# Filter loads in one hardware queue in order of use, and the start-up reordered around them, in a fused FFT filter and SwiGLU kernel

## The chip, the cores and the metric

The kernel runs on one core of one Trainium2 chip. The metric is the device time of one execution in microseconds (us). Inside a trace, times count from the start of the span.

Engines: PE is TensorE, DVE is VectorE, ACT is ScalarE, POOL is GpSimd, SP is SyncE, which here only issues DMAs.

## The reference

Eight sequences of 3008 rows of 256 numbers are filtered in the frequency domain. Then each row is normalized and goes through a gated feed-forward layer.

```python
X = np.fft.rfft(x, axis=1)                       # x: 8 x 3008 x 256
y = np.fft.irfft(X * (filt_r + 1j * filt_i), n=3008, axis=1)
x = y.reshape(8 * 3008, 256)
xn = x / np.sqrt(np.mean(x * x, -1, keepdims=True) + 1e-06) * rms_g
g, val = xn @ w_gate, xn @ w_val                 # 256 x 1536 each
out = (silu(g) * val) @ w_out                    # 1536 x 256
```

## The kernel before

The feed-forward matmuls fill PE, which was busy for 99% of the profiled span. The filter of the next sequence is fitted in beside them, but the filter of the first sequence has nothing to hide behind. This **start-up** is what the change rearranges. It goes: load x; a first transform; transposes (`t1_mm`) and copies of their results (`t1_copy`); the second transform (`stage_b`, into PSUM tiles `psb`); products with the filter (`products`); the inverse (`inverses`, into PSUM tiles `pgt`) and its copies to `gT`; second transposes; the norm; and then the first **gate product** on PE.

The filters lie in four groups, with eight frequencies in each partition; each group has a real part `fr[c]` and an imaginary part `fi[c]`. A load writes one half of the partitions, and a copy (`f_dup`) brings the same data to the other half.

```python
def f_load(c, e, eng):          # e: 0 real, 1 imaginary; three DMAs, four for c == 0
    ...
    eng.dma_start(t[p0 + 16:p0 + 63:2, :, :]..., raw(src, ...))          # 24 rows, L506
    for g in range(2):
        eng.dma_start(t[p0 + 1 + 24 * g:p0 + 24 + 24 * g:2, lo:KC, :],   # 12 rows, L509
                      raw(src, ...))
    ...
def f_dup(c, e, eng, lo=0, hi=KC):
    t = (fr, fi)[e][c][:, lo:hi, :]
    a, o = (0, HALF) if e else (HALF, 0)
    if eng is nc.scalar:
        eng.activation(out=t[a:a + HALF], in_=t[o:o + HALF], func=AXT.Copy)   # L519
    elif eng is nc.sync:
        eng.dma_start(t[a:a + HALF], t[o:o + HALF])                           # L521
    else:
        eng.tensor_copy(out=t[a:a + HALF], in_=t[o:o + HALF])                 # L523
```

The inverse writes two PSUM banks for a pair of units. When the pair is complete, the banks are copied out, by ACT for most pairs. Only then can PE start the next pair (in the profile it waited 1.97 us for such a copy before its matmul at 28.02), and these copies stand in ACT's queue among all its other work:

```python
def bit_unit(i):                # called by inverses()
    ...
    if closing:
        for dh in range(2):
            ...
            if pair > 5 and dh:
                nc.vector.tensor_copy(out=dst, in_=src)                       # L579
            else:
                nc.scalar.activation(out=dst, in_=src, func=AXT.Copy)         # L581
```

The order that the kernel before has (A is ACT, G is POOL, S is SP):

```python
for c in range(4):
    f_load(c, 0, nc.sync)
    f_load(c, 1, nc.gpsimd if c < 3 else nc.sync)
...
for g in range(4):
    t1_mm(g)
    t1_copy(g, g == 1)          # second argument: on ACT
stage_b(0, 1, 2, 3)
for g in range(4, 8):
    t1_mm(g)
f_dup(0, 0, A, 0, 2)
f_dup(0, 1, G, 0, 2)
...
f_dup(3, 0, S)                  # the last real group's copy, by DMA
products(4, 7)
f_dup(2, 0, A, 0, 4)
f_dup(2, 0, A, 4, 8)
inverses(2)
...
f_dup(3, 1, A, 0, 4)            # the last imaginary group, first half
...
inverses(6)
f_dup(3, 1, A, 4, 8)            # second half
inverses(7)
```

Of the kernel before, what the change touches and what calls it, by code (L numbers as in the profile page):

```python
# [10 lines left out]
FP32 = mybir.dt.float32  # L11
# [110 lines left out]
def kernel(  # L122
# [11 lines left out]
    nc = tc.nc  # L134
# [16 lines left out]
    up = ctx.enter_context(tc.tile_pool(name="up", bufs=2))  # L151
# [76 lines left out]
    def b_mm(b, i):  # L228
        ps = bank(3 if b else (0, 3, 4, 5)[i % 4], "psb").rearrange("p (a d) -> p a d", a=2)
        if b == 0 and i > 3:  # L230
            nc.tensor.matmul(ps[:, 0, :], wz[:, 0:P], wz[:, 0:D], start=True, stop=True)
        for u in range(2):
            k = 2 * i + u
            if b:
                w, t = late_p["wb"], st[b]["t2"][k // KC][:, k % KC, :]
            else:
                w, t = wbp, st[0]["t2"][k // 4][:, k % 4, :]
            nc.tensor.matmul(ps[:, u, :], w[:, k, :], t, start=True, stop=True)  # L238
        return ps
# [4 lines left out]
    def b_unit(b, i, ps=None):  # L244
        if ps is None:
            ps = b_mm(b, i)
        f1, f2 = filt(2 * i, 2)
        if b:
            s1 = late_p["sp"].tile([P, 2, D], FP16, tag="s1", name="s1")
            s2 = late_p["sp"].tile([P, 2, D], FP16, tag="s2", name="s2")  # L250
            if summed(b, i):
                nc.vector.tensor_tensor(out=s1, in0=ps, in1=f1, op=ALU.mult)  # L252
                st[b]["s"][i] = (s1, s2, ps, f2)
                return
        elif i % 2:
            s1 = hp.tile([P, 512], FP16, tag="sg", name="sg").rearrange("p (a d) -> p a d", a=2)
            s2 = hhs[(i // 2) % 4].rearrange("p (a d) -> p a d", a=2)
        else:
            ss = xnp.tile([P, 2, 512], FP16, tag="xn", name="ss")
            s1, s2 = (ss[:, e, :].rearrange("p (a d) -> p a d", a=2) for e in range(2))  # L260
        eng = nc.vector
        if (i in (3, 5, 8, 12, 15)) if b else (i in (3, 7, 9, 12)):
            eng = nc.gpsimd
            v = yp.tile([P, 2, 512], FP32, tag="y", name="v")
            v = v[:, 0, :].rearrange("p (a d) -> p a d", a=2)
            nc.scalar.activation(out=v, in_=ps, func=AXT.Copy)
            ps = v
        eng.tensor_tensor(out=s1, in0=ps, in1=f1, op=ALU.mult)
        eng.tensor_tensor(out=s2, in0=ps, in1=f2, op=ALU.mult)  # L269
        st[b]["s"][i] = (s1, s2)  # L270
# [229 lines left out]
    def raw(src, row, ap):  # L500
        return bass.AP(tensor=src.tensor, offset=src.offset + row * D, ap=ap)

    def f_load(c, e, eng):
        lo = 1 if c == 0 else 0
        src, t, p0 = ((filt_r, fr[c], 0), (filt_i, fi[c], HALF))[e]
        eng.dma_start(t[p0 + 16:p0 + 63:2, :, :].rearrange("p a d -> p (a d)"),  # L506
                      raw(src, c * KC, [[64 * D, 24], [1, KC * D]]))
        for g in range(2):
            eng.dma_start(t[p0 + 1 + 24 * g:p0 + 24 + 24 * g:2, lo:KC, :],  # L509
                          raw(src, 64 * (1 + 11 * g) - c * KC - lo,  # L510
                              [[64 * D, 12], [-D, KC - lo], [1, D]]))
        if c == 0:
            eng.dma_start(t[p0 + 1:p0 + 48:2, 0, :], raw(src, 32, [[64 * D, 24], [1, D]]))
# [10 lines that stand above are left out]
# [13 lines left out]
    def t1_mm(g):  # L537
        if g < 6:
            if g % 2 == 0:
                st[0]["t2t"] = t2p.tile([KR, KC, D], FP16, tag="t2", name="t2")  # L540
            dst = st[0]["t2t"][:, 4 * (g % 2):4 * (g % 2) + 4, :]
        else:
            dst = t3p.tile([KR, 4, D], FP16, tag="t3", name="t2")
        st[0]["t2"][g] = dst
        pool, tag = ((psG, "pg"), (psV, "pv"))[g % 2]
        ps = pool.tile([P, 4, D], FP16, tag=tag, name="pt1")
        af = aT.rearrange("p a k -> p (a k)")
        for a in range(4):
            for dh in range(2):
                b0 = dh * H * P  # L550
                src = af[:, b0:b0 + 32 * P].rearrange("p (i k) -> p k i", k=K2)[:, 4 * g + a, :]
                nc.tensor.transpose(ps[:, a, ts(dh, P)], src, ident)
        st[0]["t2ps"][g] = ps

    def t1_copy(g, on_act):
        dst, ps = st[0]["t2"][g], st[0]["t2ps"].pop(g)
        if on_act:
            nc.scalar.activation(out=dst, in_=ps[0:KR], func=AXT.Copy)
        else:
            nc.vector.tensor_copy(out=dst, in_=ps[0:KR])  # L560
# [60 lines left out]
        for i in range(n):  # L621
            nc.tensor.matmul(pw, wz[:, 0:P], wz, start=True, stop=True)

    def gate(ap):

        g = up.tile([1, 1], FP32, tag="gate", name="gate")
        nc.gpsimd.tensor_copy(out=g, in_=ap)

    def w_load(q):
        cols = ts(q, DFF // 3)  # L630
        for src, dst in ((moe_w_gate, wg), (moe_w_val, wv)):
            nc.gpsimd.dma_start(dst[:, :, cols], src.rearrange("(dt p) j -> p dt j", p=P)[:, :, cols])
        nc.gpsimd.dma_start(wo[:, ts(q, JT // 3), :],
                            moe_w_out.rearrange("(jt p) d -> p jt d", p=P)[:, ts(q, JT // 3), :])

    with tc.manual_schedule():
# [28 lines left out]
            zero(fi[c][HALF:P])  # L665
        with nc.allow_non_contiguous_dma(reason="one gain a partition"):
            nc.sync.dma_start(gsb, moe_rms_g.rearrange("(a p) -> p a", p=P))
        for c in range(4):
            f_load(c, 0, nc.sync)
            f_load(c, 1, nc.gpsimd if c < 3 else nc.sync)  # L670

        warm_up(14, 1)
        for g in range(4):
# [11 lines left out]
        A, G, S = nc.scalar, nc.gpsimd, nc.sync  # L685
        st[0]["t2ps"], st[0]["g"], psb = {}, {}, {}

        def products(*units):
            for i in units:
                b_unit(0, i, psb.pop(i))  # L690

        def stage_b(*units):
            for i in units:
                psb[i] = b_mm(0, i)

        def inverses(*units):
            for i in units:
                bit_unit(i)

        for g in range(4):  # L700
            t1_mm(g)
            t1_copy(g, g == 1)
        stage_b(0, 1, 2, 3)
        for g in range(4, 8):
            t1_mm(g)
        f_dup(0, 0, A, 0, 2)
        f_dup(0, 1, G, 0, 2)
        f_dup(0, 0, A, 2, 4)
        f_dup(0, 1, G, 2, 8)
        t1_copy(4, 1)  # L710
        f_dup(0, 0, G, 4, 8)
        products(0)
        stage_b(4)
        products(1)
        stage_b(5)
        t1_copy(5, 1)
        f_dup(1, 1, G)
        products(3)
        f_dup(1, 0, A, 0, 4)
        f_dup(1, 0, A, 4, 8)  # L720
        inverses(0, 1)
        products(2)
        t1_copy(6, 0)
        t1_copy(7, 0)
        stage_b(6, 7)
        f_dup(2, 1, G)
        f_dup(3, 0, S)
        products(4, 7)
        f_dup(2, 0, A, 0, 4)
        f_dup(2, 0, A, 4, 8)  # L730
# [199 lines left out]
```

## Time and profile before

| | before |
|---|---|
| time, median of 3 runs | 887.42 us (886.8 to 888.33) |
| span of the profiled run | 884.9 us |
| first product on DVE | 21.40 us |
| DVE's last product ends | 37.74 us |
| first gate product on PE | 46.25 us |
| last imaginary group landed | 30.74 us |

ACT's timeline. Columns: start, length, engine, line, operation, output and input tiles, shape, count, and in brackets how long the engine sat idle just before, and on whom.

```profile
25.07 2.00 ACT L519 ACTIVATE fr<-fr 64x1024 f32<-64x1024 f32 x2 [0.72 <-DMA fr<-in_filt_r_dram]
28.48 2.00 ACT L519 ACTIVATE fr<-fr 64x1024 f32<-64x1024 f32 x2
31.89 1.06 ACT L519 ACTIVATE fi<-fi 64x1024 f32<-64x1024 f32 x1
```

The second view is the chain of waits (start, length, what).

```profile
31.89 1.06 ACT fi L519
32.95 0.48 ACT v L266
33.43 0.75 ACT gT L581 x2
34.18 0.94 ACT fi L519
35.12 0.76 ACT gT L581 x2
```

From 31.89 on, the chain is ACT's queue: half of the filter group, a PSUM tile for POOL, two bank copies, the other half, two bank copies. DVE's products are not in these lines (the chain has three of them earlier, from 28.07 to 29.88). The SP queue's issue of the last load, three DMAs:

```profile
24.53 0.77 SPq L506 DMA_DIRECT2D fi<-in_filt_i_dram  x1
25.35 1.63 SPq L509 DMA_DIRECT2D fi<-in_filt_i_dram  x2
```

An issue takes about 0.8 us, so the third starts at 26.20.

### The profile page before, as it was taken

Reading aid. Unit: us, or ns where it says so; the run is one execution under the profiler, and the core shown is the slowest. Engines: PE = TensorE matmul, PEld = TensorE weight load, DVE = VectorE, ACT = ScalarE, POOL = GpSimd, SP = SyncE. Lnnn points to the kernel's source line nnn. Section 1 sums busy time; section 2 is a strip of 40 time slices with the busy share of each in tenths; the row PEclk is TensorE's granted clock in tenths of the full one; section 3 lists DMA queues with packets and bytes.
Section 4 is the critical chain, followed back from the end, with each engine's and each line's share of the span. In section 5 each row is a group of like instructions: output and inputs, shape, how many; then the busy total and the mean of one; then the engine's idle time right before and its main releaser. Section 6 shows DMA issues by size and latency. Waiting matters only on the chain.

```text
span 884.9 us, 17466 instructions
## 1 busy us (share of the span) xinstructions
PE 873.1 (99%) x6257; PEld 559.7 (63%) x6257; DVE 678.2 (77%) x1086; ACT 625.1 (71%) x1070; POOL 437.9 (49%) x394
## 2 busy tenths in 40 slices
PE   9799999999999999999999999999999999999997
PEld 6666666666666666766666666666666666666556
DVE  7866777899888877888688887888778887555555
ACT  7877667687677766876677766887667765676444
POOL 7844931646536752676237661376515761155300
PEclk9999999999999999999999999999999999999999
DMA  8696826665643466444735346332443233222202
GB/s 201 125 192 157 169 74 211 143 145 123 191 121 84 106 147 162 104 96 104 197 79 138 84 96 184 95 84 83 104 147 77 66 87 75 73 66 49 72 24 49
DMA packets 80096, 101.44 MB, mean 115 GB/s; under 512 B 8109, under 2 KB 56685, under 8 KB 79561
## 3 DMA queue, kind: packets, MB, share of 16 engines
q1 hardware_dynamic: 69688, 84.23, 34.7%
q0 software_dynamic: 10240, 15.96, 11.7%
q8 instruction: 49, 0.80, 0.4%
q14 instruction: 39, 0.31, 0.1%
q10 hardware_dynamic: 80, 0.13, 0.1%
HBM read 67.67 MB, written 46.78 MB: 129 GB/s over the span
## 4 chain that ended last, share of the span: by engine, by line
PE 94%; DMA 2%; DVE 1%; ACT 1%; POOL 1%; issue 1%; SPq 0%; ACTq 0%; POOLq 0%
PE po L462 27%; PE pg L443 27%; PE pv L443 27%; PE psi L291 3%; PE psb L238 3%; PE psn L323 2%; PE psa L203 2%; DMA fr<-in_filt_r_dram 2%; PE psq L352 1%; POOL xc L188 0%; DVE o L472 0%; ACT gT L581 0%; PE pt L592 0%; DVE hh L448 0%; ACT fi L519 0%
## 5 line engine op out<-in xcount | busy, mean ns | idle before, releaser
L448 DVE TENSOR_TENSOR hh<-pv,sg 128x512 f16<-128x512 f32 (+2 forms) x588 | 392.8, 670 | 188.9 <-ACT sg L447 78.1
L447 ACT ACTIVATE sg<-pg 128x512 f16<-128x512 f32 (+2 forms) x588 | 340.9, 580 | 221.1 <-PE pg L443 211.0
L462 PE MATMUL po<-wo,hh 128*128 128x256 f16 x2244 | 342.2, 272 | 0.7 <-DVE hh L448 0.3
L443 PE MATMUL pv<-xn,wv 128*128 128x512 f16 (+2 forms) x1176 | 339.6, 370 | 0.0
L443 PE MATMUL pg<-xn,wg 128*128 128x512 f16 (+2 forms) x1176 | 339.5, 370 | 0.0
L462 PEld LDWEIGHTS <-hh 128*128 128x128 f16 x2256 | 216.4, 98 | 95.5 <-issue 1.5
L282 POOL TENSOR_TENSOR s<-s,s 128x512 f16<-128x512 f16 x101 | 116.8, 1157 | 231.9 <-DVE s L276 161.3
L443 PEld LDWEIGHTS <-wv 128*128 128x128 f16 x1176 | 114.9, 98 | 128.8 <-issue 0.3
L419 POOL TENSOR_TENSOR xn<-y,rb 128x1024 f16<-128x1024 f32 (+1 forms) x45 | 126.2, 2803 | 43.8 <-DMA rb<-r_tmp 42.5
L443 PEld LDWEIGHTS <-wg 128*128 128x128 f16 x1176 | 111.3, 98 | 13.4 <-issue 0.3
L358 POOL TENSOR_TENSOR rho<-u,mhalf 128x4 f32<-128x4 f32 (+1 forms) x48 | 49.0, 1022 | 62.2 <-DVE u L356 62.0
L296 ACT ACTIVATE t<-psi 96x512 f16<-96x512 f32 x112 | 66.4, 593 | 8.3 <-PE psi L291 3.0
L276 DVE TENSOR_TENSOR s<-psb,fi 64x512 f16<-64x512 f32 x101 | 69.1, 685 | 3.1
L278 DVE SCALAR_TENSOR_TENSOR s<-psb,fi 64x512 f16<-64x512 f32 x101 | 70.0, 693 | 1.4
L329 ACT ACTIVATE y<-psn,gsb 128x512 f32<-128x512 f32 (+1 forms) x94 | 63.8, 679 | 8.1 <-PE psn L323 0.9
L252 DVE TENSOR_TENSOR s<-psb,fr 128x512 f16<-128x512 f32 x101 | 68.8, 681 | 0.0
L343 POOL TENSOR_TENSOR sq<-sq 128x512 f16<-128x512 f16 (+1 forms) x35 | 39.6, 1132 | 37.1 <-ACT sq L335 37.1
L335 ACT ACTIVATE sq<-psn 128x512 f16<-128x512 f32 (+1 forms) x94 | 54.8, 583 | 0.0
L208 ACT ACTIVATE t<-psa 128x512 f16<-128x512 f32 x70 | 41.8, 597 | 5.6 <-PE psa L203 2.1
L291 PE MATMUL psi<-s,wi 128*128 128x256 f16 x238 | 44.3, 273 | 0.0
L238 PE MATMUL psb<-t,wb 96*128 96x256 f16 x224 | 43.0, 272 | 0.3 <-DVE s L269 0.2
L323 PEld LDWEIGHTS <-t 128*128 128x128 f16 x368 | 28.4, 98 | 20.6 <-issue 0.4
(106 smaller groups left out, 527.3 us busy)
## 6 DMA issues: line engine op xcount, KB each, us to landing
out_dram<-o SPq DMA_DIRECT2D x83, 256.0 KB
xc<-in_x_dram POOLq DMA_DIRECT2D x56, 192.0 KB, 6.1
z_tmp<-t SPq DMA_DIRECT2D x28, 384.0 KB
t<-z_tmp SPq DMA_DIRECT2D x28, 384.0 KB
g_tmp<-t SPq DMA_DIRECT2D x56, 192.0 KB
rb<-r_tmp SPq DMA_DIRECT2D x41, 256.0 KB
t<-g_tmp SPq DMA_DIRECT2D x21, 384.0 KB
t<-g_tmp SPq DMA_DIRECT2D x7, 320.0 KB
```

The source lines that it names most:

```text
L238: nc.tensor.matmul(ps[:, u, :], w[:, k, :], t, start=True, stop=True)
L252: nc.vector.tensor_tensor(out=s1, in0=ps, in1=f1, op=ALU.mult)
L276: nc.vector.tensor_tensor(out=s2[a], in0=ps[e], in1=f2[e], op=ALU.mult)
L278: nc.vector.scalar_tensor_tensor(out=s2[a], in0=ps[e], scalar=-1.0, in1=f2[e], op0=ALU.mult, op1=ALU.mult)
L282: nc.gpsimd.tensor_tensor(out=s, in0=s1, in1=s2, op=ALU.add)
L291: nc.tensor.matmul(ps[:, u, :], wi_at(q, 2 * i + u), ss[q][:, u, :], start=(q == 0), stop=(q == n - 1))
L296: nc.scalar.activation(out=st[b]["t3"][c][:, 2 * r:2 * r + 2, :], in_=ps[0:KR], func=AXT.Copy)
L419: nc.gpsimd.tensor_tensor(out=xv, in0=yv, in1=rv.unsqueeze(1).to_broadcast([P, 2, n, P]), op=ALU.mult)
L443: nc.tensor.matmul(ps[:, 0:w], wt[:, dt_, ts(jt, P)], xn[:, dt_, :], start=(dt_ == 0), stop=(dt_ == 1))
L447: nc.scalar.activation(out=sg[:, 0:w], in_=pg[:, 0:w], func=AXT.Silu)
L448: nc.vector.tensor_tensor(out=hh[:, 0:w], in0=pv[:, 0:w], in1=sg[:, 0:w], op=ALU.mult)
L462: nc.tensor.matmul(po[s4 // per][:, s4 % per, :], hh[:, ts(s4, P)], wo[:, jt, :], start=(jt == 0 and s4 % per == 0), stop=(jt == JT - 1 an ...
```

## The change

The intent is to bring the filter groups in the order in which they are used, from one queue, so that the products begin earlier; to start those products between the transposes instead of after them; and to cut the last filter copy by DMA in two, so that the first half lands sooner. The diff, without the removed helper that nothing calls:

```diff
-        for c in range(4):
-            f_load(c, 0, nc.sync)
-            f_load(c, 1, nc.gpsimd if c < 3 else nc.sync)
+        f_load(0, 0, nc.sync)
+        f_load(0, 1, nc.gpsimd)
+        f_load(1, 1, nc.sync)
+        f_load(1, 0, nc.sync)
+        f_load(2, 1, nc.sync)
+        f_load(2, 0, nc.sync)
+        f_load(3, 0, nc.sync)
+        f_load(3, 1, nc.sync)
...
-        for g in range(4):
-            t1_mm(g)
-            t1_copy(g, g == 1)
-        stage_b(0, 1, 2, 3)
-        for g in range(4, 8):
-            t1_mm(g)
+        t1_mm(0)
+        t1_copy(0, 0)
         f_dup(0, 0, A, 0, 2)
         f_dup(0, 1, G, 0, 2)
+        t1_mm(1)
+        stage_b(0, 1)
         f_dup(0, 0, A, 2, 4)
         f_dup(0, 1, G, 2, 8)
-        t1_copy(4, 1)
+        t1_copy(1, 1)
+        t1_mm(2)
+        t1_mm(3)
         f_dup(0, 0, G, 4, 8)
         products(0)
+        stage_b(2, 3)
+        products(1)
+        t1_copy(2, 0)
...
-        f_dup(3, 0, S)
+        f_dup(3, 0, S, 0, 4)
+        f_dup(3, 0, S, 4, 8)
```

More of the change, by code (lines that the diff above doesn't have):

```diff
@@ L622, in warm_up @@
             nc.tensor.matmul(pw, wz[:, 0:P], wz, start=True, stop=True)
-    def gate(ap):
-        g = up.tile([1, 1], FP32, tag="gate", name="gate")
-        nc.gpsimd.tensor_copy(out=g, in_=ap)
     def w_load(q):
@@ L698, in inverses @@
                 bit_unit(i)
-        for g in range(4):
-            t1_mm(g)
-            t1_copy(g, g == 1)
-        stage_b(0, 1, 2, 3)
-        for g in range(4, 8):
-            t1_mm(g)
+        t1_mm(0)
+        t1_copy(0, 0)
         f_dup(0, 0, A, 0, 2)
         f_dup(0, 1, G, 0, 2)
+        t1_mm(1)
+        stage_b(0, 1)
         f_dup(0, 0, A, 2, 4)
         f_dup(0, 1, G, 2, 8)
-        t1_copy(4, 1)
+        t1_copy(1, 1)
+        t1_mm(2)
+        t1_mm(3)
         f_dup(0, 0, G, 4, 8)
         products(0)
+        stage_b(2, 3)
+        products(1)
+        t1_copy(2, 0)
+        for g in range(4, 7):
+            t1_mm(g)
         stage_b(4)
-        products(1)
-        stage_b(5)
-        t1_copy(5, 1)
         f_dup(1, 1, G)
         products(3)
+        t1_copy(4, 1)
+        t1_copy(5, 1)
+        products(2)
+        t1_copy(3, 0)
+        t1_mm(7)
+        stage_b(5)
         f_dup(1, 0, A, 0, 4)
@@ L721 @@
         inverses(0, 1)
-        products(2)
+        stage_b(6)
         t1_copy(6, 0)
         t1_copy(7, 0)
-        stage_b(6, 7)
+        stage_b(7)
         f_dup(2, 1, G)
-        f_dup(3, 0, S)
+        f_dup(3, 0, S, 0, 4)
+        f_dup(3, 0, S, 4, 8)
         products(4, 7)
```

## The prediction

The sum stands: DVE's last product at 37.5 us against 37.74, a gain of about 0.2 us. The first landing at 19.7 is the author's estimate, close to the landing of the same group's third piece (19.73), and that other loads had held up the last piece was not shown. What the trace of the kernel before shows is this: eleven completion records of that last piece came from 18.55 to 19.43 and the last at 20.63; and from 16 to 20 us, with both queues at work, the DMA moved 199 to 213 GB/s, which is 0.20 to 0.21 MB per us. Part 2 counts "waits for the eighth transfer before": in that trace SP began issues at 18.41, 19.35 and 22.39, each 0.02 us after the eighth transfer before it had landed (18.39, 19.33, 22.37). The argument for the second rival took such a lag of a piece's last record for constant, but in the last imaginary group of that trace it was 0.25 to 0.69 us, not 1.20.

> **What bounds the kernel now.** I read the busy shares first, then the chain of waits to find how far the start-up reaches, then the engines' timelines inside it.
>
> ```profile
> span 884.9 us, 17466 instructions
> PE 873.1 (99%) x6257; PEld 559.7 (63%) x6257; DVE 678.2 (77%) x1086; ACT 625.1 (71%) x1070; POOL 437.9 (49%) x394
> PE 94%; DMA 2%; DVE 1%; ACT 1%; POOL 1%; issue 1%; SPq 0%; ACTq 0%; POOLq 0%
> ```
>
> PE is busy for 99% and carries 94% of the chain; the other 6% lies almost wholly ahead of the first gate product, which the PE timeline has at 46.25 us. From there to 884.9 us PE runs without holes, and the change touches no line of that part. So **the change is worth what it moves the first gate product**, one for one. Inside the start-up, windows of five microseconds:
>
> ```profile
> 20.00:25.00 5.00, 4.42 (x64) 4.01 (x63) 4.55 (x8) 3.76 (x6) 4.75 (x5) 1.00 0.85 203
> 25.00:30.00 5.00, 2.54 (x33) 1.91 (x30) 5.00 (x10) 4.88 (x7) 4.86 (x4) 1.00 0.61 140
> 30.00:35.00 5.00, 4.49 (x58) 3.52 (x59) 4.48 (x8) 4.95 (x9) 4.95 (x5) 1.00 0.52 109
> ```
>
> The columns are stretch, length, busy time of PE, its weight loads, DVE, ACT, POOL, then clock, DMA share and GB/s. Between 25 and 35 us PE is the idle one; DVE, ACT and POOL are all full, while the DMA has room. The reader should see three engines at the limit together: time taken from one of them alone is worth little. Now the DVE line by line, whose products end the stage:
>
> ```profile
> 18.62 0.69 DVE L560 COPY t<-pt 96x1024 f16<-96x1024 f16 x1 [0.75 <-PE pt L552]
> 19.66 1.28 DVE L560 COPY t<-pt 96x1024 f16<-96x1024 f16 x2 [0.35 <-PE pt L552]
> 21.40 0.69 DVE L268 TENSOR_TENSOR ss<-psb,fr 128x512 f16<-128x512 f32 x1 [0.45 <-ACT fr L519]
> ...
> 25.00 1.28 DVE L560 COPY t<-pt 96x1024 f16<-96x1024 f16 x2
> ...
> 34.06 0.69 DVE L268 TENSOR_TENSOR sg<-psb,fr 128x512 f16<-128x512 f32 x1 [0.39 <-PE pgt L573]
> ...
> 37.06 0.68 DVE L269 TENSOR_TENSOR hh<-psb,fi 128x512 f16<-128x512 f32 x1
> ```
>
> The products begin at 21.40, after a wait for ACT's copy of the first real filter group to the other half of the partitions, and end at 37.74. Of the 16.34 us, 24 products at a pitch of 0.60 us are 14.4 and two transposed-tile copies (the pair at 25.00) 1.2, so only about 0.7 us are gaps. Three such copies ran before 21.40, when DVE had nothing else to do. That ACT copy waited for the load:
>
> ```profile
> 20.73 1.17 ACT L519 ACTIVATE fr<-fr 64x512 f32<-64x512 f32 x2 [0.56 <-DMA fr<-in_filt_r_dram]
> 19.00 0.57 POOL L509 DMA_DIRECT2D fi<-in_filt_i_dram  x1 [1.39 <-DMA fi<-in_filt_i_dram]
> 19.61 2.05 POOL L523 COPY fi<-fi 64x512 f32<-64x512 f32 x2
> 22.88 1.89 POOL L523 COPY fi<-fi 64x2048 f32<-64x2048 f32 x1
> ```
>
> POOL is held until 19.57 by issuing loads of later imaginary groups. The completion records in the trace put the landing of the first groups at 20.63 (real) and 19.16 (imaginary). [...]
>
> [...]
>
> **The change, part by part.**
>
> 1. **Filters into one queue.** It takes six load issues (second and third imaginary group) of 0.54 to 0.63 us from POOL, 3.5 us, all before 19.57 and beside its waiting. POOL can start its first copy when the imaginary group lands, 19.2 instead of 19.61: 0.4 us earlier. [...] I estimate the landing at 19.7 instead of 20.63. ACT then needs the 0.67 us that now lie between 20.73 and the product at 21.40, so the first product can start at about 20.4, **1.0 us earlier**. The floor is about 19.8: the imaginary group, and first transposes, their copy and two matmuls.
> 2. **The later groups.** The SP queue issues a piece in about 0.8 us, a group of three in 2.4. Waits for the eighth transfer before included, I estimate the issue of the last filter piece at 28.6 (before 26.20) and landings of: second imaginary 21.5, second real 23, third imaginary 25, third real 27, fourth real 29, fourth imaginary 31.4. Their users come at about 22.4 (POOL), 25 (ACT), 26.6 (POOL), 28.8 (ACT), 29.4 (SP) and 31.6 (ACT). Each is in time, the last by little.
> 3. **Copies between products.** All eight tile copies stay on their engines. But of the DVE's three early ones, two now stand after the first products: 2 x 0.60 = **1.2 us come into the full stretch**. ACT's copy of tile 1 (1.02 us) likewise goes behind its first filter copies, against 0.72 us of idle time before 25.07 that goes.
> 4. **Last filter copy in two DMAs.** Before, one 512 KB copy was issued at 29.37 and its increments came at 33.3 to 33.9. The product at 34.06 began then; the 0.39 us before it stands under PE in the view, but that inverse had issued long before, so I put it down to this copy. Halves of 256 KB should land near 32.5 and 33.6, ahead of the users at about 34 and 35: **up to 0.4 us** goes.
> 5. The removed one-element copy helper is never called: nothing.
>
> Sum for DVE: start at 20.4; 24 x 0.60 = 14.4; four copies 2.4; new and old small gaps 0.3 (a wait for the last transposes, which in turn wait for the copy that frees their bank). 20.4 + 14.4 + 2.4 + 0.3 = 37.5, against 37.74. The stretch behind it (inverses, second transposes, norm, first gate product: 8.5 us) is unchanged. **Gain about 0.2 us**, 887.42 to 887.2. POOL's last product ended at 36.90 and should end near 36.3; it isn't the end of the chain.
>
> **Rivals.**
>
> - *The early filter is all that counts.* If the first landing comes down to the floor, products start at 19.9 and end at 37.0: 0.7 us gained, 886.7. For it: the waits at 20.73 and 21.40 show that only data was missing. Against it: x itself was landing until 15.85[...].
> - *The copies cancel or reverse it.* If the landing doesn't move[...], products start at 21.4 as before, with 1.2 us more work behind them: 38.4, so 888.1. [...]
> - *The single queue becomes the bound.* Issue at 2.4 us a group[...] could make the last imaginary group late: ACT's copy at about 31.6 is tight. One or two microseconds late would show at the end as about 0.5 to 1.5 us, 888 to 889. Against it: from the third real group to the fourth imaginary one the trace has a group landing every 1.5 to 2.0 us from that queue alone.
> - *It is all hidden.* ACT and POOL are as full as DVE between 25 and 35 us, so an early product only waits for filter copies later: no change, 887.4.
>
> **Range and chances.** The mechanisms give -0.7 to +1.5 us; the three runs before spread over 886.8 to 888.33. As a change of this kind was likely made because something measured better, I lean slightly below my sum: 887.1, with 885.9 to 888.5 to hold it 8 times in 10. Two per cent are 17.7 us, more than a third of the whole start-up of 46 us, which is out of reach; so within 2% has 0.98.
>
> **What would show it.** Right: the first product on DVE near 20.4 with its wait still for a filter copy; the pair of copies at 19.66 gone and four copies among the products; no wait for a DMA before the product at 34; DVE's last product at 37.0 to 38.0, first gate product within 0.7 us of 46.25. Wrong, if the first product starts before 19.8 or after 21.2; if ACT's copies of the last imaginary group, or POOL's of the second, wait for DMA by over 0.5 us; or if PE shows holes after the first gate product that it hadn't before, which nothing here would explain.

## More of the kernel before

After its first copy ACT waits once, for the second real group, and begins to copy the last imaginary group at 31.89. It doesn't wait there: the group had landed at 30.74.

## The result, and the profile after

| | before | after |
|---|---|---|
| time, median of 4 runs | 887.78 (886.80 to 888.33) | 889.35 (887.98 to 889.75) |
| span of the profiled run | 884.9 | 887.4 |
| first product on DVE | 21.40 | 20.36 |
| last imaginary group landed | 30.74 | 33.53 |
| ACT begins to copy it | 31.89 | 33.61 |
| DVE's last product ends | 37.74 | 38.75 |
| first gate product on PE | 46.25 | 48.75 |
| span less first gate product | 838.65 | 838.65 |

The ratio of the two is 1.0016, with a 95% interval of 0.9999 to 1.0033. A ratio here is the mean time of one kernel's fast runs over that of the other's of the same rounds, so it is not quite the ratio of the medians in the table. In a later set, five runs of the changed kernel had a median of 890.2 against 886.93 of eleven runs before, ratio 1.0028 (1.0016 to 1.0040). So the change costs about 2 us: within 2 per cent, but slower (shown by the second interval; the first still holds 1), and outside the range that was predicted. The profiled runs differ by 2.50 us at the first gate product and by nothing behind it. First the line of the kernel before, then that of the changed one:

```profile
46.25 0.38 PE L443 MATMUL pg<-xn,wg 128*128 128x512 f16 x1
48.75 0.38 PE L443 MATMUL pg<-xn,wg 128*128 128x512 f16 x1
```

The part behind that product isn't equal in every trace: in the 14 of this document it is 838.6 to 839.0 us, but 839.4 in e3_fill and 840.3 in before_again. So the time of a single run depends on more than its start-up.

The page of the changed kernel, its span and busy shares:

```profile
span 887.4 us, 17469 instructions
PE 874.3 (99%) x6257; PEld 561.0 (63%) x6257; DVE 678.1 (76%) x1086; ACT 624.8 (70%) x1070; POOL 434.2 (49%) x388
```

These say nothing of the loss: the busy times are those of before within 1.3 us, but for POOL's, which are 3.7 us lower. The loss is only seen inside the start-up. DVE's timeline:

```profile
20.36 0.69 DVE L268 TENSOR_TENSOR ss<-psb,fr 128x512 f16<-128x512 f32 x1 [1.23 <-ACT fr L519]
...
34.58 0.69 DVE L268 TENSOR_TENSOR sg<-psb,fr 128x512 f16<-128x512 f32 x1 [0.45 <-PE pgt L573]
...
36.87 0.69 DVE L269 TENSOR_TENSOR ss<-psb,fi 128x512 f16<-128x512 f32 x1 [0.30 <-ACT fi L519]
```

The first product begins 1.04 us earlier, as intended. The wait near 34 is still there, and at 36.87 DVE waits for ACT's copy of the last imaginary group, which it didn't before. So to ACT's timeline:

```profile
19.69 1.16 ACT L519 ACTIVATE fr<-fr 64x512 f32<-64x512 f32 x2 [2.31 <-DMA fr<-in_filt_r_dram]
20.88 1.02 ACT L558 ACTIVATE t<-pt 96x1024 f16<-96x1024 f16 x1
22.58 0.61 ACT L266 ACTIVATE v<-psb 128x512 f32<-128x512 f32 x1 [0.69 <-PE psb L238]
...
29.20 2.00 ACT L519 ACTIVATE fr<-fr 64x1024 f32<-64x1024 f32 x2 [0.79 <-DVE hh L269]
...
33.61 1.06 ACT L519 ACTIVATE fi<-fi 64x1024 f32<-64x1024 f32 x1 [1.01 <-DMA fi<-in_filt_i_dram]
```

ACT also starts 1.04 us earlier (19.69 against 20.73). Then it has the tile copy at 20.88, which before lay ahead of its filter copies, and three waits. The one at 29.20 is put down to DVE by the view, but the third real group had landed at 29.10, so I take it as a wait for that load. The wait at 22.58 is a new round trip, as PE's own line shows:

```profile
21.95 0.60 PE L238 MATMUL psb<-t,wbp 96*128 96x256 f16 x4 [1.19 <-ACT t L558]
```

PE waits for ACT's tile copy to make the next second transforms, and ACT waits for these: that is the 0.69 us. And the chain of waits of the changed kernel, where before's had ACT alone:

```profile
28.85 4.68 DMA fi<-in_filt_i_dram
33.53 0.03 ACTq L519
33.56 0.04 issue
33.61 0.06 ACT fi L519
```

The last load's final piece is issued at 28.85 (before 26.20), lands at 33.53, and ACT starts at once. Behind it the chain is the same as before: one `v`, two `gT`, the second half of `fi`, two `gT`.

**The balance of ACT's queue.** From the start of the first filter copy to that of the last imaginary group's copy I take off the time in which ACT waited for loads. What is left is how long this stretch takes with all data there:

| | first copy | waits for loads | rest | last copy |
|---|---|---|---|---|
| before | 20.73 | 0.72 | 10.44 | 31.89 |
| after | 19.69 | 0.79 + 1.01 | 12.12 | 33.61 |

The new order lengthens ACT's stretch by 1.68 us: 1.02 for the tile copy and 0.69 for the round trip, 1.71 together. The early start (-1.04) plus the longer stretch (+1.68) plus the change in load waits (1.80 - 0.72 = +1.08) make +1.72, which is the shift of the last copy.

That leaves 0.78 us of the 2.50, behind this copy: from it to the first gate product the kernel before took 14.36 us, the changed one 15.14. The windows show it. I cut them to 3.41 us, the length of the halved stretch in the changed kernel: there up to its start and from it on, and in the kernel before, whose clock took no such step in the start-up, a stretch at a like place. The columns are those of the prediction's windows. First the kernel before, then the changed one:

```profile
34.35:37.76 3.41, 2.09 (x37) 1.66 (x36) 3.39 (x6) 2.65 (x7) 3.41 (x5) 1.00 0.03 7
```

```profile
33.64:37.06 3.42, 1.70 (x24) 1.14 (x22) 2.66 (x5) 3.42 (x6) 3.37 (x4) 1.00 0.39 85
37.06:40.47 3.41, 3.16 (x37) 2.88 (x36) 1.69 (x3) 2.16 (x6) 3.41 (x5) 0.50 0.27 30
```

In the changed kernel PE's clock is halved from 37.06 to 40.47, right behind a stretch in which PE was busy for 1.70 of 3.42 us, and just where the inverses run. Such halvings also fell on other stretches and on the kernel before, at other places in each trace: 22.30 to 25.71 in a second one of the changed kernel (after_again), 30.50 to 33.91 in a second one of the kernel before (before_again). PE's busy time ahead of them does not tell where they fall: it was 2.05 of 3.41 us before the halving in e4, while in the kernel before a stretch with 1.92 (24.12 to 27.53) was followed by full clock.

### The profile page after: what moved, and what is told of

The parts are those of the page before. It is cut to its first block, busy times and chain, and to the rows that moved or that the text cites. A ratio compares the mean times of both kernels' runs of the same rounds, so it can differ in the third digit from the quotient of the medians.

```text
span 887.4 us, 17469 instructions
## 1 busy us (share of the span) xinstructions
PE 874.3 (99%) x6257; PEld 561.0 (63%) x6257; DVE 678.1 (76%) x1086; ACT 624.8 (70%) x1070; POOL 434.2 (49%) x388
## 4 chain that ended last, share of the span: by engine, by line
PE 94%; DVE 1%; DMA 1%; POOL 1%; ACT 1%; issue 1%; SPq 0%; DVEq 0%; ACTq 0%; POOLq 0%
PE po L462 27%; PE pg L443 27%; PE pv L443 27%; PE psi L291 3%; PE psb L238 3%; PE psn L323 2%; PE psa L203 2%; DMA fr<-in_filt_r_dram 1%; PE psq L352 1%; DMA fi<-in_filt_i_dram 1%; POOL xc L188 0%; DVE o L472 0%; PE pt L592 0%; ACT gT L581 0%; SPq L509 0%
## 5 line engine op out<-in xcount | busy, mean ns | idle before, releaser
L443 PEld LDWEIGHTS <-wg 128*128 128x128 f16 x1176 | 111.3, 98 | 13.4 <-issue 0.3
```

Of the source, the lines that this page charges most:

```text
L443: nc.tensor.matmul(ps[:, 0:w], wt[:, dt_, ts(jt, P)], xn[:, dt_, :], start=(dt_ == 0), stop=(dt_ == 1))
```

## The experiments

**Theory at the start:** the end of the start-up is set by ACT's queue, not by DVE, and in the changed kernel the last imaginary load holds that queue up; the halved clock adds to it. **Rivals:** the new compute order costs the time by itself; or the halved clock is the main cause; or the load is late only because DMA bandwidth is short, so that no queue would help. The first rival became half of the answer. Where a quotation names a theory by a letter, the sentence ahead of it here says in words what was asked.

All trace readings are put together here: one look each, in the order of the section. "Rest" is as above. "To gate" runs from ACT's copy of the last imaginary group to the first gate product. "Halved" is the stretch of halved clock, if any fell between 18 and 46 us.

| run | order | first copy | load waits | rest | last copy | to gate | first gate | halved |
|---|---|---|---|---|---|---|---|---|
| before | old | 20.73 | 0.72 | 10.44 | 31.89 | 14.36 | 46.25 | none |
| after | new | 19.69 | 1.80 | 12.12 | 33.61 | 15.14 | 48.75 | 37.06-40.47 |
| e1_queue_only | old | 20.10 | 2.62 | 10.55 | 33.27 | 14.36 | 47.63 | 29.10-32.52 |
| e2_order_only | new | 20.06 | 0 | 12.19 | 32.25 | 14.35 | 46.60 | none |
| e3_fill | new | 20.67 | 1.16 | 12.17 | 34.00 | 14.36 | 48.36 | none |
| e4_fr3_act_queue | new | 20.32 | 2.08 | 12.22 | 34.62 | 15.35 | 49.97 | 38.98-42.40 |
| e5_fr3_pool_old_order | old | 21.36 | 0.82 | 10.44 | 32.62 | 14.35 | 46.97 | 30.74-34.15 |
| e6_fr3_pool | new | 19.39 | 1.97 | 12.14 | 33.50 | 14.35 | 47.85 | 33.96-37.38 |
| e7_fr3_pool_fill | old | 21.59 | 2.85 | 10.39 | 34.83 | 14.35 | 49.18 | 31.12-34.53 |
| e8_two_pieces_only | old | 20.80 | 0.94 | 10.44 | 32.18 | 14.35 | 46.53 | 29.78-33.19 |
| e9_fi3_half_by_dma | old | 20.79 | 0.53 | 10.43 | 31.75 | 14.15 | 45.90 | 29.57-32.98 |
| e10_no_last_load | new | 18.78 | 1.20 | 12.26 | 32.24 | 14.36 | 46.60 | none |
| after_again | new | 20.54 | 0 | 12.92 | 33.46 | 14.36 | 47.82 | 22.30-25.71 |
| before_again | old | 21.11 | 0.68 | 10.44 | 32.23 | 14.36 | 46.59 | 30.50-33.91 |

Two things hold throughout: "rest" is 10.39 to 10.55 us in the seven with the old order and 12.12 to 12.92 in the seven with the new one. And the last imaginary group landed at 30.15 to 32.13 in the five with the old loads, at 33.20 to 33.93 in the four with the new loads unaltered. The tail is lengthened in the two traces in which the halved stretch lies over the last inverses: in the changed kernel it begins 3.45 us behind the start of the copy and in e4 4.36 us. In e6 it begins 0.46 us behind it, and the tail is 14.35 us. (The waits of e4 and e5 include 0.17 and 0.82 us which the view puts down to other instructions, but a load that the copy needed had landed about 0.1 us before.)

### The queue alone

The kernel before with the new loads and nothing else. It asks whether the loads alone bring the late landing.

```diff
 (kernel before)
-        for c in range(4):
-            f_load(c, 0, nc.sync)
-            f_load(c, 1, nc.gpsimd if c < 3 else nc.sync)
+        f_load(0, 0, nc.sync)
+        f_load(0, 1, nc.gpsimd)
+        f_load(1, 1, nc.sync)
+        ... (the changed kernel's eight lines)
```

> The kernel before with the filter loads moved into one queue and nothing else. Theory A (the SP queue issues a piece every 0.85 us, so the seven groups it now carries end with the last imaginary piece issued at about 28.9 us and landed at about 33.5, and the copy of the last real group can't be issued before 31.2): first product at about 20.9 instead of 21.40 us, ACT's last filter copies wait for DMA until about 33.5, the product near 34 waits until about 35, DVE's last product ends at about 38.7 instead of 37.74; time 1 to 2.5 us over before. Rival B (the copies among the products cost the time, the queue is a gain): products end at about 37.2 and the time is 0.5 us under before.

Measured: median 888.43 (887.7 to 889.42), ratio 1.0014 (1.0002 to 1.0026). ACT's timeline at the end of its stretch:

```profile
30.33 0.60 ACT L266 ACTIVATE v<-psb 128x512 f32<-128x512 f32 x1
33.27 1.06 ACT L519 ACTIVATE fi<-fi 64x1024 f32<-64x1024 f32 x1 [2.34 <-DMA fi<-in_filt_i_dram]
```

ACT was ready at 30.93, a microsecond before the kernel before's 31.89, and then waited 2.34 us for a group that landed at 33.20. The early filter was fully won and more than fully given back at the last load. So the loads alone make a loss, and the place of it is this wait.

### The order alone

The changed kernel's compute order with the queues and the one-piece copy of before. It asks whether the order costs anything when loads come as they did.

```diff
 (changed kernel)
-        f_load(0, 0, nc.sync)
-        ... (the eight lines)
+        for c in range(4):
+            f_load(c, 0, nc.sync)
+            f_load(c, 1, nc.gpsimd if c < 3 else nc.sync)
...
-        f_dup(3, 0, S, 0, 4)
-        f_dup(3, 0, S, 4, 8)
+        f_dup(3, 0, S)
```

> The changed kernel's order of copies and products, with the old queues and the one-piece copy. Theory A: first product at 21.4 us as before (the first real filter lands at about 20.6), two copies of 0.6 us more in the full stretch, no wait for the last filters; DVE's last product ends at 38.5 to 38.9, about 1 us over before. Rival B (the reordering costs nothing, ACT and POOL set the pace anyway): 37.7 and the time of before. Both parts being over before alone would say that the change pays two prices, not one.

Measured: median 888.79, but the six runs go from 886.62 to 890.64; ratio 1.0016 (1.0001 to 1.0031). The trace is of one of the quicker runs (887.25):

```profile
32.25 1.05 ACT L519 ACTIVATE fi<-fi 64x1024 f32<-64x1024 f32 x1
```

ACT never waited for a load after its first copy at 20.06, and still arrived 0.36 us later than in the kernel before, because its stretch took 12.19 us instead of 10.44. So the order has a cost of its own on ACT, 1.75 us in these two traces, which in this one an earlier first copy (20.06 against 20.73) and the missing wait (0.72) nearly made good. DVE's last product ended at 38.10, earlier than the 38.5 to 38.9 expected. How much of the loss in the medians belongs to the order the spread of the runs leaves open.

### Filling PE's pause, and one load from ACT's queue

The first adds nine dummy matmuls to the one that stands before the last second transform, in PE's pause ahead of the halved stretch. It asks whether the halved stretch goes with the pause, and what it is worth.

```diff
 (changed kernel, in b_mm)
         if b == 0 and i > 3:
-            nc.tensor.matmul(ps[:, 0, :], wz[:, 0:P], wz[:, 0:D], start=True, stop=True)
+            for _ in range(10 if i == 15 else 1):
+                nc.tensor.matmul(ps[:, 0, :], wz[:, 0:P], wz[:, 0:D], start=True, stop=True)
```

> The changed kernel with nine more dummy matmuls ahead of the last forward matmul pair, in a stretch where PE waits anyway (34.3 to 35.5 us). Theory C (the granted clock halved from 37.06 to 40.47 us[...], and about 1.5 us of the 2.5 us loss is that): no stretch of 0.5 clock near 37 us, first gate product at about 47.3 instead of 48.8 us, time about 1.5 us under the changed kernel, about 0.5 to 1 us over before. Rival D (the late filters make the whole loss and the clock record is without effect or of other cause): first gate product stays near 48.8.

Measured: median 889.04 (888.04 to 889.76), ratio 1.0020 (1.0008 to 1.0032). The window over the former pause:

```profile
35.72:39.13 3.41, 2.61 (x41) 2.20 (x39) 3.04 (x5) 2.65 (x7) 3.41 (x4) 1.00 0.02 5
```

No halved stretch fell into this start-up, and the tail is 14.36 us again instead of 15.14, so the clock was worth 0.8 us there. That the filling kept the clock up is not shown by it: e2 and e10, without filling, had no halved stretch there either. The time is no better than the changed kernel's, whose ratios are 1.0016 and 1.0028: the expected gain was missed. In this trace the first real group landed at 20.56 instead of 19.59, with the same loads, and ACT waited 1.16 us for the last group (landed 33.93). A further 0.8 us of this run's time lies behind the first gate product. The clock is a part of the loss in the first trace, not its cause.

The second moves the last real group to ACT's hardware queue, to tell the pace of issue on SP from a limit in the transfers behind it: in the first case the groups land earlier, in the second (the rival in the quotation) they don't.

```diff
 (changed kernel)
-        f_load(3, 0, nc.sync)
...
         warm_up(2, 0)
+        f_load(3, 0, nc.scalar)
```

> The changed kernel with the three loads of the last real group issued from ACT's own hardware queue, in the 2.3 us in which ACT waits for the first filter. Theory A1 (issue on one queue is the limit): every group behind it lands one group earlier, the last imaginary one at about 31.1 instead of 33.5; the copy of the last real group is issued at about 27 and lands near 30.5; no wait for either; DVE's last product at about 37.8, no halved clock, first gate product at about 46.3; time within 0.7 us of before. Rival A2[...]: the groups land no earlier than in the changed kernel within 0.5 us, and the time stays near 889.3.

Measured: median 890.14 (889.3 to 890.64), ratio 1.0031 (1.0018 to 1.0044). The test failed, because the move changed more than was meant: SP's second piece of an earlier group was now held until 16.73, its last issue came at 30.37 instead of 28.85, and the last group landed at 34.54. It says nothing on issue against transfers.

### One load from POOL's queue

Instead, the last real group goes to POOL's queue, behind the first imaginary group: in the old order (e5), in the new order (e6), and in the old order with dummy matmuls before units 7 and 15 (e7). They ask whether fewer issues on SP bring the last group earlier, and whether that is paid for by the first groups. The third asks whether, with two of PE's pauses filled, no halved stretch is left and the runs lie closer together.

```diff
 (e5: e1_queue_only; e6: changed kernel; the same move)
         f_load(0, 1, nc.gpsimd)
+        f_load(3, 0, nc.gpsimd)
...
-        f_load(3, 0, nc.sync)
 (e7: e5, and in b_mm)
+            for _ in range({7: 9, 15: 7}.get(i, 1)):
```

> The kernel before (its order of work, its one-piece copy) with the other loads in one queue in order of use, but the last real group on the GpSimd queue behind the first imaginary one, so that the last imaginary group is issued one group earlier. Theory E (the start-up ends 14.36 us after ACT starts its copy of the last imaginary group, as in four traces; ACT reaches that copy at about 30.9 us with the queue change, and only the late load, at 33.2, held it): load landed at about 30.5, ACT's copy at 30.9 to 31.3 against 31.89 before, first gate product at 45.3 to 45.7, time 0.5 to 0.9 us under before. Rival F (DVE's products set the end): DVE's last product at about 37.2 whatever ACT does, first gate product 45.7 at best and later if the product near 34 waits for its filter copy. Rival G (the load on the GpSimd queue takes bandwidth from the first groups): first product after 21.2 us and the time of before.

> The changed kernel with the same one move, the last real group to the GpSimd queue. Theory E: ACT no longer waits for the last imaginary group and starts its copy at about 32.6 us instead of 33.61 (its own earlier work is 0.7 us later than before); first gate product at 46.9 to 47.0 with a full clock, up to 0.8 more with a halved one; time 1 to 1.8 us under the changed kernel and still about 0.7 us over before. Rival (the late load doesn't matter): first gate product stays at 48.4 to 48.8.

> The run with the last real group on the GpSimd queue and the old order, with 8 and 6 more dummy matmuls ahead of two forward pairs (units 7 and 15), where PE waits anyway. Theory C[...]: no halved stretch in the start-up, and the runs lie closer together, within 1 us instead of 2.4, with a median about 0.5 us lower than the same without fill. Rival D: the same spread and median as without fill.

Measured on one chip, with before at 887.5 (885.97 to 892.05): e5 888.79, ratio 1.0009 (0.9991 to 1.0027); e6 889.97, ratio 1.0023 (1.0005 to 1.0041); e7 888.21, ratio 0.9998 (0.9977 to 1.0020). In e5 the last imaginary group landed at 31.57, early enough, but the first copy moved to 21.36, and what was won at the end was lost at the start. That the moved load took bandwidth from the first groups is not shown: with the same loads the first real group landed at 21.26 in e5 and 21.48 in e7, but at 19.29 in e6. In e6 the last group was issued 1.5 us earlier than in the changed kernel (27.31) and landed only 0.5 us earlier (33.02), and ACT lost its time one group before:

```profile
30.09 2.00 ACT L519 ACTIVATE fr<-fr 64x1024 f32<-64x1024 f32 x2 [1.78 <-DMA fr<-in_filt_r_dram]
```

So the wait moved to the third real group, which landed at 29.98. In e7 the clock was still halved for one stretch (31.12 to 34.53), ACT waited 2.85 us for loads in its trace, and the runs were spread from 885.77 to 890.07: the filling narrowed nothing. The dummy matmuls ran at 26.3 to 27.2 and at 35.9 to 36.6, so none of them lay in the 3.41 us ahead of the halving, in which PE was busy for 1.83 us (27.71 to 31.12). None of the three beats the kernel before.

### The two-piece copy alone, and half of the last copy by DMA

The kernel before with only the cut of the last real group's copy (e8), and the same with the second half of the last imaginary group's copy taken from ACT and given to SP (e9). The first asks for the effect of the change's third part. The second takes a piece out of ACT's tail: if ACT's queue sets the end, the gate product comes earlier.

```diff
 (e8: kernel before)
-        f_dup(3, 0, S)
+        f_dup(3, 0, S, 0, 4)
+        f_dup(3, 0, S, 4, 8)
 (e9: e8, and)
+        f_dup(3, 1, S, 4, 8)
...
-        f_dup(3, 1, A, 4, 8)
```

> The kernel before with only the last filter copy cut in two. Theory E: the product near 34 us no longer waits (33.7 instead of 34.06) and DVE's last product ends near 37.4 instead of 37.74, but ACT's copy of the last imaginary group still starts at about 31.9, so the first gate product stays at 46.2 to 46.3 and the time is that of before. Rival F (DVE's products set the end): first gate product 0.3 to 0.4 us earlier.

> The kernel before with the last real group's copy in two pieces and, new, the second half of the last imaginary group's copy by a third such DMA in place of ACT. Theory E (the end of the start-up hangs on ACT's queue: filter copies, then the copies that free PE's banks): ACT's string behind its first copy of that group is 0.95 us shorter, so first gate product 13.4 to 13.7 us after the start of that copy instead of 14.35, at about 45.3 to 45.8 us, time 0.5 to 0.9 us under before, products of units 14 and 15 without a wait if the third piece lands by 35.5. Rival F (DVE's products set the end): DVE's last product stays at 37.4 to 37.8 and the first gate product within 0.3 us of 46.25.

Measured: e8 886.77 (885.82 to 887.72), ratio 0.9986 (0.9968 to 1.0004); e9 886.65 (885.14 to 888.82) against 886.93, ratio 0.9993 (0.9979 to 1.0006). Neither is shown faster or slower. In e8 the halves were issued at 29.32 and 29.93 and landed at 32.32 and 33.52, where the single copy of before had landed at 33.89. The product near 34 no longer waits, as expected, but DVE's last product ended at 38.45 instead of about 37.4, after a wait of 1.06 us at 32.38 that the view puts down to ACT. ACT's tail is 14.35 us, as before. So the early half moves nothing, since the end isn't set there: DVE ended 0.71 us later than in the kernel before and the gate product came 0.28 us later, as ACT's copy did (32.18 against 31.89).

In e9 the last imaginary copy started at 31.75 and the gate product came at 45.90: 14.15 us instead of 14.36, and not the 13.4 to 13.7 expected. About 1 us of ACT's work was taken out and only 0.2 us came off. ACT's queue is thus not the only limit of the tail; another, close behind it, took over. The view shows ACT waiting 0.46 us for the inverses at 34.65, and the chain of waits runs through PE's second transforms and inverses from 29.97 to 36.26. PE's clock was halved from 29.57 to 32.98 in this trace, so how much would come off at full clock is open.

### Without the last load, and both kernels once more

The changed kernel without the load of the last imaginary group. Its result is wrong (relative error 0.50). It asks whether the loss goes when nothing has to land there. With it, both kernels were run again unchanged.

```diff
 (changed kernel)
-        f_load(3, 1, nc.sync)
```

> The changed kernel without the load of the last imaginary group (its place keeps zeros, so the result is wrong on purpose; all else as in the changed kernel). Theory E: ACT starts its copy of that group when its own work lets it, at about 32.6 us instead of 33.61; first gate product 14.35 us later, at about 47.0 (a halved clock would add 0.8 to 1); time 1 to 1.8 us under the changed kernel and still about 0.7 over before, which is what the new order of copies costs ACT. Rival (the lateness of that load is not the cause): first gate product stays at 48.4 to 48.8.

> The changed kernel once more, for a second trace and five more times on the chip of the other two. Theory: ACT's copy of the last imaginary group waits for its load until 33 to 34 us; first gate product 14.35 us later at full clock or up to 1 us more at a halved one, at 47.5 to 49; time 1 to 2.5 us over before. If the first trace was a chance one, the copy starts at 32 to 32.6 and the time is within 0.5 us of before.

> The kernel before once more, for a second trace. Theory: last imaginary group landed at 30.5 to 31 us, ACT's copy of it starts without a wait for it at 31.7 to 32.3, first gate product 14.35 us later, at 46.0 to 46.7; the spread of that start between the two traces tells how much of the 0.7 us by which ACT's own work was later in the changed kernel is chance.

Measured on one chip, with before at 886.93 (885.81 to 888.69, 11 runs): e10 887.39 (886.7 to 888.11), ratio 1.0002 (0.9991 to 1.0014); the changed kernel 890.2 (888.47 to 890.35), ratio 1.0028 (1.0016 to 1.0040); the kernel before as a test of the method 886.98, ratio 0.9992 (0.9978 to 1.0007). Without the last load nearly the whole loss is gone, so this load, by ACT's wait or by its share of the traffic, is needed for it. It isn't gone in a simple way, though. In e10's trace ACT started its first copy at 18.78, earlier than in any other run. That isn't the removed load's doing, which the changed kernel issues only from 27.20 on, so I put it down to chance. ACT then waited for the third real group:

```profile
28.83 2.00 ACT L519 ACTIVATE fr<-fr 64x1024 f32<-64x1024 f32 x2 [1.20 <-DMA fr<-in_filt_r_dram]
```

An early start had turned into a wait for the next group. DVE ended its products at 37.44 there, 0.30 us earlier than in the kernel before, and the gate product came at 46.60, 0.35 us later: this is the plainest sign that DVE doesn't set the end. In e9 it is the other way round: DVE ended at 38.24, 0.49 us later than in the kernel before, and the gate product came 0.35 us earlier.

The trace of after_again is of its fastest run (888.47). ACT didn't wait for the last load there, which landed at 33.39, because it was late itself: its first group landed at 20.43, and the clock was halved from 22.30 to 25.71, amid its stretch, which took 12.92 us instead of 12.2. The first gate product came at 47.82, 0.93 us before that of the first trace. So the single parts differ from run to run, and in part their sum too.

The trace of before_again is of its slowest run (888.93), and it missed its expectation: the kernel before waited for its last load here.

```profile
32.23 1.06 ACT L519 ACTIVATE fi<-fi 64x1024 f32<-64x1024 f32 x1 [0.68 <-DMA fi<-in_filt_i_dram]
```

The group landed at 32.13, not at 30.5 to 31 us, and the gate product came at 46.59, 0.34 us later than in the first trace. ACT's stretch without load waits was 10.44 us in both. So the wait for the last load is no fixed difference of the two kernels: each had it in one of its two traces. The longer stretch on ACT is one: 10.44 us in both traces of the kernel before, 12.12 and 12.92 in those of the changed one.

## Why the prediction was wrong

It foretold 887.1 with 885.9 to 888.5; the medians were 889.35 and 890.2. A gain of some tenths was expected and a loss of about 2 us came. By its own steps:

- **"The change is worth what it moves the first gate product"**: right. Behind that product both profiled runs took 838.65 us, and no new holes came.
- **Step 1, the first product at about 20.4 and the landing at 19.7**: right in the profiled run, 20.36 and 19.59. It isn't as firm as that: in the five traces with these loads up to there (after, after_again, e1, e3, e10) the group landed at 18.68 to 20.56, and in the five with the old loads at 19.96 to 21.01. The gain is there in the mean, 0.85 us, but the two ranges overlap.
- **The DVE line, "whose products end the stage"**: this is the step that failed first. I took DVE as the bound, with about 0.7 us of gaps, though I had written that time taken from one engine alone is worth little. My windows were misread too: from 30 to 35 us ACT and POOL are at 4.95 of 5.00 us, DVE only at 4.48, and PE, which I called the idle one, at 4.49. The gate product follows ACT's copy of the last imaginary group by 14.35 to 14.36 us in every run but the two with a late halved stretch and e9, which cuts this copy. In the same runs it follows DVE's last product by anything from 8.1 to 9.2 us, and POOL's last product by 8.9 to 10.3. The chain of waits of the kernel before already had ACT there, from 31.89 on, and I did not read it at that place.
- **Step 3, the copies**: the four copies did come among DVE's products, but its stretch from first to last product became 18.39 us, not the 17.1 of the sum, with ACT's late filter copy in it. For ACT I set the tile copy of 1.02 us against an idle 0.72 us that would go, and took this for an even trade. It left out the round trip of 0.69 us through PE, and waits for loads did not go. The new order makes ACT's stretch 1.7 us longer (12.2 against 10.44, in the table), which is more than the early start brings.
- **Step 2, "each is in time, the last by little"**: wrong, and the term of it is the time from issue to landing. The last issue was foretold at 28.6 and came at 28.85. The landing was foretold at 31.4 and came at 33.53. I had allowed 2.8 us, while this very piece took 4.5 in the kernel before (26.20 to 30.74); in the changed one it took 4.7. The second imaginary group landed as foretold, at 21.59 against 21.5. Then groups came every 2.4 us, close to the issue of a group in 2.54, where I had put 1.5 to 2.4.
- **Step 4, the last copy in two**: wrong. The halves landed at 34.40 and 35.75, not 32.5 and 33.6, for the last real group landed at 31.11, not 29, and so they were issued at 31.19 and 31.80. The wait near 34 stayed: 0.39 us before, 0.45 after. e8 has the halves near the times that I foretold, and it gains nothing that its interval could show.
- **What was not foreseen at all** is the halved clock, 0.78 us in the profiled run.

In the sum for the profiled runs: -1.04 for the early start, +1.68 for the order on ACT, +1.08 for load waits, +0.78 for the clock: 2.50, as measured. The rival "the single queue becomes the bound" gave 888 to 889 and was nearest. I gave it too little weight, because of the spacing of 1.5 to 2.0 us between the last landings in the kernel before; in the changed kernel, with seven groups in this queue, it was 2.0 to 2.7. "It is all hidden" was right for e10's early start.

**What stays open:** how much of the last group's lateness is the pace of issue and how much the transfers themselves. The pace has a share: in the changed kernel SP issues a piece every 0.85 us without a pause from 18.69 to the last at 28.85. In e1 the last three groups landed 2.8 to 3.5 us after their last issue, so the transfers were not far behind there; in e6 it was 5.7 to 6.3, so there they were. With the 3.5 us of e1 the last group of the changed kernel would have landed at about 32.4 by my estimate, just before ACT was ready for it at 32.60. Also open is how much of e2's loss in the medians is chance, what halves the clock where it is halved, and why the part behind the first gate product is longer in before_again and e3.

## What to carry to other kernels

Before you trust an engine's nearly gapless timeline as the bound, follow the chain of waits at the end of the stage, and look for the engine whose queue of work frees the buffers that others need; count what a reorder adds to that queue, round trips included. When loads are put into one queue, take the time from issue to landing for the same piece from the trace (4.5 us here before, 4.7 after), and add up issues to the last one, since an early first landing can be lost again at the last one, as in e1 (first copy 0.63 us earlier, last copy 1.38 later). Look at the granted clock of each stretch of a start-up too: here a stretch in which PE was busy for 1.70 of 3.42 us was followed by one of halved clock that cost 0.78 us, though it isn't shown that the one brought the other.
